# Threshold attention before a squared-ReLU layer: Prelu as the threshold, the exponential behind the turn, and value products with the turned weights as the stationary block

## The chip, the cores and the metric

The kernel runs on one core of one Trainium2 chip. A time is the device time of one execution in microseconds (us), and a kernel's time is the median of its runs. The engines are called PE (TensorE, matrix products; PEld is its loading of stationary blocks), DVE (VectorE), ACT (ScalarE), POOL (GpSimd) and SP (SyncE, which only issues DMAs here). A "fill" below is one LDWEIGHTS, the loading of a stationary block into PE's array; the other operand, which runs through the array, is the streamed one. A "turn" is a transposition done by PE.

## What is computed

```
q, k, v: (8, 8, 576, 64)          # batch, heads, positions, width
scores = q @ k^T / 8
scores = where(scores >= max(scores) - tau, scores, -1e9)       # tau = 0.02
attn   = exp(scores - max(scores));  attn /= (sum(attn) + 1e-9)
x      = (attn @ v), heads side by side: (4608, 512)
h      = max(x @ w_in, 0)                                       # w_in (512, 2048)
out    = (h * h) @ w_out                                        # w_out (2048, 512)
```

The weights w_in and w_out come as 64-bit numbers and are made into 32-bit ones on the chip. Everything else is 32-bit floating point.

## The kernel before

The program has an attention stage and then the two layers, whose products are cut up by a Strassen-like scheme. The change touches the attention stage alone.

Two heads are handled together, one on partitions 0 to 63 and one on 64 to 127 (`j` is the head of the pair). A pair of heads has 576 query rows, which are cut into four blocks of 128 rows and a rest of 64; the rests of two pairs share one block. Each such block is a **unit**, 144 in all, and two units, A and B, make a **period**, 72 in all. The steps of a period are issued in an order written out by hand: `PLAIN` (line 623), `CONVERTING` (line 628) for the periods that also make a block of 32-bit weights (steps c1 to c6), and two lists for the first periods. A dash behind a step's name puts it one period late, so that every engine always has work of several units. Each engine works its instructions off in the order of this list.

For a unit PE multiplies turned q by turned k (`scores`, line 448) into six of the eight PSUM banks, called `sc`: 512 columns and a rest of 64 for each head, cut into blocks of 64 rows and 64 columns of the array, four of which work side by side. DVE copies the negated scores out and takes their minimum on the way (`top`, 475). POOL adds tau (`least`, 483). ACT takes the exponential of the copy (`power`, 486), DVE multiplies it by the threshold's mask and sums it (`mask`, 491), and POOL and DVE make the inverse of the sum (`over`, `inverse`).

The weights of both units must then be turned, since a product sums over partitions. PE turns 18 blocks a period (`fill`, 524) in three parts, V and U into the pool `pt` of two banks and W into banks of `sc`; ACT copies them to the tile `wT` (`filled`, 545). PE also spreads the inverse sums over columns (`spread_sums`, 532). `values` (554) then has a block of V stationary, 64 rows and 64 columns, four side by side, and streams 128 columns of `wT` through it. The product comes out already turned, as the layers want it; ACT and DVE take it out (`values_out`, 701), with the division by the sums there or on POOL (`given_out`, 715).

Turned q and k come from PE as well (`turn`, 414), into banks 1 and 4, with ACT taking them out. q, k and v are asked for by SP some periods ahead. `touch` (378) orders instructions that meet in a PSUM bank.

Of the kernel before, what the change touches and what calls it, by code (L numbers as in the profile page):

```python
# [48 lines left out]
def kernel(  # L49
# [63 lines left out]
    tau_p = const.tile([P, 1], FP32, name="tau_p")  # L113

    def read_tau():
# [4 lines left out]
        nc.vector.tensor_scalar(out=tau_p[:, :], in0=tau_c[:, :], scalar1=0.0, scalar2=None, op0=ALU.max)  # L120
# [250 lines left out]

    touched = deque()
    behind = mybir.DependencyInfo(mybir.DependencyClass.Sync, mybir.DependencyReason.DATA)

    Q_RING, K_RING, W_RING = 3, 4, 2
    MEET = (("scores", "turnedq", (Q_RING,)), ("scores", "turnedk", (K_RING,)), ("last scores", "turnedk", (K_RING,)), ("values", "weights", (W_RING,)), ("last values", "last weights", (W_RING,)), ("x", "weights", (W_RING,)))

    def touch(what, made, at, size, key=0):

        if at is None:  # L380
            return
        on = range(at // BANK, (at + size - 1) // BANK + 1)
        met = {made.ins.engine}
        for kind, other, others, its in reversed(touched):
            e = other.ins.engine
            if e == made.ins.engine:
                continue
            if on[-1] < others[0] or others[-1] < on[0]:
                if any({what, kind} == {x, y} and any((key - its) % n == 0 for n in rings) for x, y, rings in MEET):
# [9 lines left out]
    def half_turn(pt, slot, of, at=None):  # L399

        for r in range(2):
            rows = ds(r * HALF, HALF)
            made = nc.tensor.transpose(pt[:, r, ts(slot, HALF)], of[rows, :], ident[rows, rows])  # L403
            touch("turns", made, at and at + r * BANK, BANK)
# [9 lines left out]
    def turn(i, which, spots, other=None):  # L414
# [5 lines left out]
        for t, x in enumerate(of):  # L420
            for r, (spot, at) in enumerate(spots):
                rows = ds(r * HALF, HALF)
                made = nc.tensor.transpose(spot[:, ts(t, HALF)], x[rows, :], ident[rows, rows])  # L423
                touch("turns", made, at, BANK)
        half, kind = FULL * HALF, "turnedk" if which else "turnedq"

        def scaled(to, spot):
            touch(kind, nc.scalar.activation(out=to, in_=spot[0], func=AF.Identity, scale=qscale[:, :]), spot[1], BANK, i)

        def then():  # L430
            part = lambda r, x, n: (spots[r][0][:, ds(x, n)], spots[r][1])
            if which:
                for r, n in ((0, half), (1, half + REST)):
                    spot = part(r, 0, n)
                    copy_by = other if r and other else nc.scalar.copy
                    touch(kind, copy_by(to[1][:, ds(r * half, n)], spot[0]), spot[1], BANK, i)
                scaled(to[2], part(0, half, REST))
                ask_ahead(i, 1)
            else:
                for r in range(2):  # L440
                    scaled(to[0][:, ds(r * half, half)], part(r, 0, half))
                ask_ahead(i, 0)
# [5 lines left out]
    def scores(n, rest):  # L448
# [3 lines left out]
        for j in range(2):  # L452
            first = n % 2 != j
            to = (3 * j + 1) * BANK + first * (BANK - REST) if rest else (3 * j + 2 * first) * BANK
            for c in range(2):
                rows, at = ds(j * D, D), ds(c * HALF, HALF)
                qT, kT, qR = turned[of[c]]
                lhs = qT[rows, ds((c * FULL + t) * HALF, HALF)] if t < FULL else qR[rows, :]
                made = nc.tensor.matmul(  # L459
                    sc[at, ds(to, count)], lhs, kT[rows, ds(at_k, count)], start=True, stop=True  # L460
                )
                touch("scores" if t < FULL else "last scores", made, to, count, of[c])

    def softmax(n):

        if n // 2 not in smalls:
            smalls[n // 2] = sb.tile([P, 4, 4], FP32, tag="small", bufs=4, name="small")
        small = smalls[n // 2]
        nmx, thr, sm = (small[:, i, ds(n % 2 * 2, 2)] for i in range(3))
        w = sb.tile([P, CH, 2, D], FP32, tag=f"w{n % 4}", name="w")  # L470
        s = sb.tile([P, 2, S], FP32, tag=f"s{n % 2}", name="s")
        weights[n] = w
        of = lambda j: s[:, j, :].rearrange("p (c d) -> p c d", d=D)

        def top(j):
            at = 3 * j * BANK + (n % 2 != j) * (2 * BANK - REST)
            made = nc.vector.tensor_scalar(  # L477
                out=s[:, j, :], in0=sc[:, ds(at, S)], scalar1=1.0, scalar2=None,
                op0=ALU.mult, op1=ALU.min, accum_out=nmx[:, j : j + 1],
            )  # L480
            touch("tops", made, at, S)
# [4 lines left out]
        def power(j):  # L486
            nc.scalar.activation(  # L487
                out=w[:, :, j, :], in_=of(j), func=AF.Exp, bias=nmx[:, j : j + 1], scale=-1.0
            )

        def mask(j):
            nc.vector.scalar_tensor_tensor(  # L492
                out=w[:, :, j, :], in0=of(j), scalar=thr[:, j : j + 1], in1=w[:, :, j, :],
                op0=ALU.is_le, op1=ALU.mult, accum_out=sm[:, j : j + 1],
            )

        def over():
            sm = small[:, 2, :]
            nc.gpsimd.tensor_scalar(out=sm, in0=sm, scalar1=1e-9, scalar2=None, op0=ALU.add)

        def inverse():
            nc.vector.reciprocal(out=small[:, 3, :], in_=small[:, 2, :])

        soft[n] = dict(top=top, least=least, power=power, mask=mask, over=over, inverse=inverse)
# [12 lines left out]
    FIRST = [(u, c) for c in range(CH) for u in range(2)]  # L517
    FILLS = {"V": (0, 8), "W": (8, 2), "U": (10, 8)}
    SCALE_AT = 10

    def weight_at(n):
        return n if n < SCALE_AT else n + 2

    def fill(m, f, pt, at=None):

        first, count = FILLS[f]
        if m not in wT:
            wT[m] = sb.tile([P, (2 * CH + 2) * P], FP32, tag="wT", bufs=W_RING, name="wT")
        for i, (u, c) in enumerate(FIRST[first : first + count]):
            half_turn(pt, i, weights[2 * m + u][:, c, :, :].rearrange("p j d -> p (j d)"), at)  # L530

    def spread_sums(m, pt, at):

        rs, count = smalls.pop(m), FILLS["W"][1]
        for j in range(2):
            for r in range(2):
                rows = ds(r * HALF, HALF)
                for u in range(2):
                    one = rs[rows, 3, 2 * u + j : 2 * u + j + 1]
                    wide = bass.AP(tensor=one.tensor, offset=one.offset, ap=[one.ap[0], [0, D]])  # L540
                    to = pt[ds(u * D, D), r, ts(count + j, HALF)]
                    made = nc.tensor.matmul(to, wide, ident[rows, rows], start=True, stop=True)  # L542
                    touch("turns", made, at + r * BANK, BANK)

    def filled(m, f, pt, at=None, last=False):

        first, count = FILLS[f]
        count += 2 * (f == "W")
        to = wT[m][:, ds(weight_at(first) * P, count * P)]
        copy_by = nc.vector.tensor_copy if last else nc.scalar.copy  # L550
        kind = "last weights" if last else "weights"
        touch(kind, copy_by(joined(to), whole(pt, 0, count)), at, 2 * BANK, m)  # L552

    def values(m):

        for c in range(CH):
            for u in range(2):
                for s, (i, _, count, row) in enumerate(halves(2 * m + u)):
                    for j in range(2):
                        rows = ds(j * D, D)  # L560
                        made = nc.tensor.matmul(  # L561
                            sc[ds(u * D, D), ds(5 * j * BANK + row, count)], loaded_v[i][rows, (c - (u != j)) % CH, :],
                            wT[m][rows, ds(weight_at(2 * c + u) * P + row, count)],
                            start=(c == 0 and s == 0), stop=(c == CH - 1), skip_group_check=True,
                        )
                        part = "first values" if c < FULL else "values" if c == FULL else "last values"
                        touch(part, made, 5 * j * BANK, BANK, m)

    def valued(m):

        for u in range(2):
            n = 2 * m + u
            weights.pop(n)
            if units[n][1] == FULL:
                for i in units[n][0]:
                    loaded_v.pop(i)
                    if i + 3 < len(pairs):
                        load_v(i + 3)
# [839 lines left out]
```

## Time and profile before

| | before |
|---|---|
| median of 3 runs | 1270.58 us (1269.65 to 1272.4) |
| profiled execution, span from first to last instruction | 1273.4 us (its time is not listed apart from the span) |
| PE busy | 1251.7 us, 98% of the span |
| DVE busy | 988.2 us, 78% |
| ACT busy | 844.3 us, 66% |
| POOL busy | 982.5 us, 77% |
| DMA | 196.79 MB, q1's packets 52.8% of 16 engines' span |
| mean granted clock of PE | 0.996 |

The busy shares are means over two unlike stages; a stage is read by itself, from a window of the trace. A row of a line gives the line of the kernel, the engine, the operation, the tiles (written <- read) and the shape: "64*128 64x64" is a stationary block of 64 rows and 128 columns and a streamed operand of 64 partitions and 64 columns. A 32-bit product is recorded as two instructions, a turn as one. Some records of PE can be missing (a few per cent).

### The profile page before, as it was taken

What the parts mean: (1) busy time and instruction counts of PE and PEld (TensorE: products, weight loads), DVE (VectorE), ACT (ScalarE), POOL (GpSimd) and SP (SyncE); (2) the same over time, 40 slices, a digit from 0 to 9 for tenths busy, and PEclk for the clock granted to TensorE, in tenths of its full rate; (3) what the DMA queues carried; (4) which work ended last, traced back from release to release, by engine and by line L of the source; (5) the groups of instructions that cost most, each with busy time, mean ns of one, the idle gap of its engine ahead of it and who ended that gap; (6) DMA issues with size and microseconds to landing.
All of it is one profiled execution on the core that took longest, in us unless ns stands there. A gap on an engine that the chain in (4) does not pass through costs nothing.

```text
span 1273.4 us, 55161 instructions
## 1 busy us (share of the span) xinstructions
PE 1251.7 (98%) x22991; PEld 1093.6 (86%) x22991; DVE 988.2 (78%) x2385; ACT 844.3 (66%) x1536; POOL 982.5 (77%) x1070
## 2 busy tenths in 40 slices
PE   8999999999999999999999999999999999999998
PEld 5777776777777778988888888999999999999998
DVE  6999998999999996886887878867746654665463
ACT  6999998999999994666765856675524432443240
POOL 2999998877776542988898989868787878787776
PEclk8999999999999999999999999999999999999999
DMA  7566677434333323657667657579965336533511
GB/s 186 143 161 154 167 198 188 120 89 107 89 81 89 83 53 97 192 166 237 202 191 231 215 169 249 172 274 369 267 163 152 83 107 163 146 84 107 167 35 35
DMA packets 289912, 196.79 MB, mean 155 GB/s; under 512 B 98560, under 2 KB 250624, under 8 KB 289664
## 3 DMA queue, kind: packets, MB, share of 16 engines
q1 hardware_dynamic: 288352, 192.86, 52.8%
q8 instruction: 181, 2.97, 1.0%
q14 instruction: 67, 0.55, 0.1%
q10 hardware_dynamic: 1312, 0.41, 0.1%
HBM read 120.85 MB, written 72.35 MB: 152 GB/s over the span
## 4 chain that ended last, share of the span: by engine, by line
PE 72%; DMA 3%; ACT 2%; POOL 2%; DVE 1%; issue 1%; DVEq 0%; ACTq 0%; POOLq 0%; SPq 0%
PE po L818 27%; PE ph L997 17%; PE ph L818 10%; PE sc L561 7%; PE sc L459 6%; PE pt L403 4%; PE sc L542 1%; PE sc L423 1%; POOL arena L126 1%; DMA g<-arena 1%; ACT arena L970 1%; DVE arena L126 1%; DMA w<-arena 1%; ACT arena L971 1%; ACT c L857 1%
## 5 line engine op out<-in xcount | busy, mean ns | idle before, releaser
L126 POOL TENSOR_TENSOR arena<-arena 128x512 f32<-128x512 f32 (+1 forms) x314 | 378.7, 1224 | 125.1 <-DVE arena L126 113.5
L818 PE MATMUL po<-wall,arena 128*64 128x128 f32 x7056 | 385.8, 273 | 1.4 <-ACT arena L813 0.8
L818 PEld LDWEIGHTS po<-wall,arena 128*64 128x64 f32 x7056 | 385.1, 137 | 1.9 <-ACT arena L813 1.0
L126 DVE TENSOR_TENSOR arena<-ph,arena 128x512 f32<-128x512 f32 x378 | 254.5, 688 | 77.4 <-PE ph L997 30.9
L123 POOL TENSOR_TENSOR arena<-arena 128x128 f32<-128x128 f32 (+1 forms) x322 | 265.5, 826 | 24.1 <-DMA arena<-w 8.5
L997 PE MATMUL ph<-arena,wall 128*128 128x256 f32 x1176 | 256.7, 380 | 2.3 <-DVE arena L126 2.1
L997 PEld LDWEIGHTS ph<-arena,wall 128*128 128x128 f32 x1176 | 222.4, 190 | 36.3 <-DVE arena L126 6.2
L126 DVE TENSOR_TENSOR arena<-po,arena 128x128 f32<-128x128 f32 x378 | 107.6, 288 | 159.3 <-PE po L818 151.4
L492 DVE SCALAR_TENSOR_TENSOR arena<-arena 128x576 f32<-128x576 f32 x288 | 225.9, 820 | 0.4 <-ACT arena L487 0.3
L487 ACT ACTIVATE arena<-arena 128x576 f32<-128x576 f32 x288 | 214.1, 781 | 13.4 <-DVE arena L477 13.3
L477 DVE TENSOR_SCALAR_CACHE_REDUCE arena<-sc 128x576 f32<-128x576 f32 x288 | 203.4, 752 | 18.5 <-ACT arena L552 5.7
L857 ACT COPY c<-arena 128x512 f32<-128x512 f32 (+1 forms) x295 | 168.9, 578 | 70.1 <-DVE arena L123 36.1
L459 PE MATMUL sc<-arena 64*64 64x512 f32 (+1 forms) x2304 | 179.6, 415 | 5.6 <-ACT arena L552 1.2
L561 PE MATMUL sc<-arena 64*64 64x128 f32 (+1 forms) x5760 | 165.6, 261 | 1.0 <-ACT arena L552 0.5
L123 DVE TENSOR_TENSOR arena<-arena,c 128x512 f32<-128x512 f32 x235 | 154.2, 664 | 12.1 <-ACT c L857 7.1
L561 PEld LDWEIGHTS sc<-arena 64*64 64x64 f32 x5760 | 150.4, 133 | 4.5 <-ACT arena L552 0.7
L552 ACT COPY arena<-pt 128x1024 f32<-128x1024 f32 x143 | 145.0, 1014 | 4.6 <-PE pt L403 3.9
L459 PEld LDWEIGHTS sc<-arena 64*64 64x64 f32 x2304 | 76.8, 134 | 71.4 <-issue 47.2
L813 ACT COPY arena<-po 128x128 f32<-128x128 f32 x63 | 16.6, 264 | 177.6 <-PE po L818 174.8
L818 PE MATMUL ph<-arena,wall 128*64 128x128 f32 x2352 | 129.2, 273 | 0.6 <-DVE arena L710 0.6
L818 PEld LDWEIGHTS ph<-arena,wall 128*64 128x64 f32 x2352 | 128.3, 137 | 1.4 <-issue 1.0
L484 POOL TENSOR_SCALAR arena<-arena,tau_p 128x2 f32<-128x2 f32 x144 | 83.8, 582 | 58.5 <-DVE arena L477 44.7
(55 smaller groups left out, 1142.5 us busy)
## 6 DMA issues: line engine op xcount, KB each, us to landing
gp<-arena SPq DMA_DIRECT2D x96, 256.0 KB, 3.4
arena<-gp SPq DMA_DIRECT2D x96, 256.0 KB, 5.4
w<-arena SPq DMA_DIRECT2D x60, 256.0 KB, 2.7
wall<-w SPq DMA_DIRECT2D x49, 256.0 KB, 5.3
g<-arena SPq DMA_DIRECT2D x48, 256.0 KB, 3.7
arena<-g SPq DMA_DIRECT2D x48, 256.0 KB, 5.0
arena<-w SPq DMA_DIRECT2D x44, 256.0 KB, 3.4
arena<-in_v_dram SPq DMA_DIRECT2D x32, 288.0 KB, 3.8
```

The source lines that it names most:

```text
L123: e.tensor_tensor(out=out, in0=x, in1=y, op=ALU.subtract)
L126: e.tensor_tensor(out=out, in0=x, in1=y, op=ALU.add)
L459: made = nc.tensor.matmul(sc[at, ds(to, count)], lhs, kT[rows, ds(at_k, count)], start=True, stop=True)
L477: made = nc.vector.tensor_scalar(out=s[:, j, :], in0=sc[:, ds(at, S)], scalar1=1.0, scalar2=None, op0=ALU.mult, op1=ALU.min, accum_out=nmx ...
L484: nc.gpsimd.tensor_scalar(out=thr, in0=nmx, scalar1=tau_p[:, :], scalar2=None, op0=ALU.add)
L487: nc.scalar.activation(out=w[:, :, j, :], in_=of(j), func=AF.Exp, bias=nmx[:, j : j + 1], scale=-1.0)
L492: nc.vector.scalar_tensor_tensor(out=w[:, :, j, :], in0=of(j), scalar=thr[:, j : j + 1], in1=w[:, :, j, :], op0=ALU.is_le, op1=ALU.mult, a ...
L552: touch(kind, copy_by(joined(to), whole(pt, 0, count)), at, 2 * BANK, m)
L561: made = nc.tensor.matmul(sc[ds(u * D, D), ds(5 * j * BANK + row, count)], loaded_v[i][rows, (c - (u != j)) % CH, :], wT[m][rows, ds(weigh ...
L818: nc.tensor.matmul(to[cols], lhs[:, cols], rhs, start=start, stop=stop, skip_group_check=True)
L857: nc.scalar.copy(c, y)
L997: nc.tensor.matmul(to[:, 2 * j : 2 * j + 2, :], W_IN[m, k][:, ts(2 * h + j, P)], part_x(steps, k, m), start=(not more and j == 0), stop=Tr ...
```

## The change

- **Threshold.** DVE's `mask` goes. `top` writes the negated scores straight into the weights' tile, and ACT's `keep` puts Prelu in its place: with x = (minimum + tau) - negated score, x stays where it is not negative and is multiplied by 2^80 where it is, which the exponential later makes zero.
- **Exponential.** It is taken when the turned blocks leave PSUM: `filled` is now ACT's Exp with bias -tau instead of a copy. The parts are V (9 - 1 = 8 blocks of unit A), U (8 of unit B) and W (the last block of each, in banks 0 and 5, taken out by two instructions).
- **Value products.** `wT` is now the stationary operand, 64 rows and 128 columns, two blocks side by side, and V with a column of ones is streamed, 65 columns. The result has the query rows on partitions, the sum of the weights in its 65th column, in banks 2 and 3.
- **Division and result.** DVE adds 1e-9 to the sums, takes the inverse and multiplies (`values_out`); the result is turned by PE (`x_turned`, four turns) and taken out by DVE (`x_out`, two copies). `spread_sums`, `over`, `inverse` and POOL's multiplication go.
- **Scores.** The blocks of 64 rows and 64 columns become 64 rows and 128 columns, except in a unit that two pairs share. Units A have banks 1 to 4 and units B banks 0, 1, 4 and 5.
- **Turned q and k** leave PSUM by DVE instead of ACT.
- **V** is loaded with a pitch of 68 numbers, a row of 64 at a time, with ones behind each (set once by POOL for each of three buffers).
- **Order.** New `PLAIN` and `CONVERTING` lists, and a table `NEEDS` that issues a step's forerunners first.

The core of the diff:

```diff
     def load_v(i):
-        va = sb.tile([P, CH, D], FP32, tag="va", bufs=3, name="va")
+        va = sb.tile([P, CH, V_PITCH], FP32, tag="va", bufs=V_RING, name="va")
+        if i < V_RING:
+            nc.gpsimd.memset(va[:, :, D : D + 1], 1.0)
         nc.sync.dma_start(
-            out=va[:, :, :].rearrange("p c d -> p (c d)"),
-            in_=v[b, h : h + 2, :, :].rearrange("j (p c) d -> (j p) (c d)", c=CH),
+            out=va[:, :, 0:D],
+            in_=v[b, h : h + 2, :, :].rearrange("j (p c) d -> (j p) c d", c=CH),
         )
...
-        def scaled(to, spot):
-            touch(kind, nc.scalar.activation(out=to, in_=spot[0], func=AF.Identity, scale=qscale[:, :]), spot[1], BANK, i)
+        def out(to, r, at, count, scale):
+            from_ = spots[:, r, ds(at, count)]
+            if scale:
+                made = nc.vector.tensor_scalar(out=to, in0=from_, scalar1=qscale[:, :], scalar2=None, op0=ALU.mult)
+            else:
+                made = nc.vector.tensor_copy(to, from_)
+            touch(kind, made, banks and banks[r : r + 1], i)
...
+            if t < FULL:
+                qT, kT, _ = turned[of[0]]
+                made = nc.tensor.matmul(
+                    sc[:, ds(to, count)], qT[rows, ts(t, P)], kT[rows, ds(at_k, count)], start=True, stop=True
+                )
+                touch("scores", made, [bank], of[0])
+                continue
...
-        def power(j):
+        def keep(j):
             nc.scalar.activation(
-                out=w[:, :, j, :], in_=of(j), func=AF.Exp, bias=nmx[:, j : j + 1], scale=-1.0
+                out=w[:, :, j, :], in_=w[:, :, j, :], func=AF.Prelu, bias=thr[:, j : j + 1], scale=-1.0, alpha=DROP
             )
-        def mask(j):
-            nc.vector.scalar_tensor_tensor(
-                out=w[:, :, j, :], in0=of(j), scalar=thr[:, j : j + 1], in1=w[:, :, j, :],
-                op0=ALU.is_le, op1=ALU.mult, accum_out=sm[:, j : j + 1],
-            )
...
-        copy_by = nc.vector.tensor_copy if last else nc.scalar.copy
-        touch(kind, copy_by(joined(to), whole(pt, 0, count)), at, 2 * BANK, m)
+        for r in ((slice(0, 2),) if banks is None else (slice(0, 1), slice(1, 2))):
+            made = nc.scalar.activation(
+                out=joined(to)[:, r, :, :], in_=whole(pt, 0, count)[:, r, :, :], func=AF.Exp, bias=below[:, :], scale=1.0
+            )
...
                         made = nc.tensor.matmul(
-                            sc[ds(u * D, D), ds(5 * j * BANK + row, count)], loaded_v[i][rows, (c - (u != j)) % CH, :],
-                            wT[m][rows, ds(weight_at(2 * c + u) * P + row, count)],
-                            start=(c == 0 and s == 0), stop=(c == CH - 1), skip_group_check=True,
+                        sc[ds(row, count), ds((2 + j) * BANK + u * X_PITCH, D + 1)],
+                        wT[m][rows, ds(at + row, count)], loaded_v[i][rows, (c - (u == j)) % CH, 0 : D + 1],
+                        start=(c == 0 and u == 0), stop=(c == CH - 1), skip_group_check=True,
...
+            made = nc.vector.tensor_scalar(
+                out=over(2), in0=both[:, :, :, D], scalar1=1e-9, scalar2=None, op0=ALU.add
+            )
+            nc.vector.reciprocal(out=small[:, 3, :], in_=small[:, 2, :])
+            made = nc.vector.tensor_tensor(
+                out=xn[:, :, :].rearrange("p u (j d) -> p j u d", j=2), in0=both[:, :, :, 0:D], in1=wide, op=ALU.mult
+            )
...
+                for u in range(2):
+                    half_turn(pt["X"], X_SLOT + u, xn[:, u, :], W_BANKS, "x turns", p)
...
+                for r in range(2):
+                    made = nc.vector.tensor_copy(x[:, :, ts(r, HALF)], whole(pt["X"], X_SLOT, 2)[:, r, :, :])
...
     PLAIN = """
-        put give fetch ahead eU-- powA0-- V-- powA1-- eV-- maskA1-- PV-- powB1-- c1- RA- powB0-- T--
-        maskA0-- U- W-- Q-- x-- c4- maskB1-- SA- eT-- RB- maskB0-- topA0- over- topA1- c2 s2 leastA- eW--
-        SB- topB0- s1- c5 c6 topB1- inv- leastB- xm-- c3
+        put give fetch ahead T RA c1 SA zA0- eT tA0 c2 W-- eU-- eW-- tA1 V- c3 SB RB zB1- tB1 c4- lA tB0 lB zB0- eV- c5- P1-- P2--
+        U- out-- c6-- X--- eX--- zA1 s1 s2
     """.split()
     CONVERTING = """
-        put give fetch ahead SB- c1 RA topB0- powA1- c2- topB1- PV- c5- powA0- maskA0- eT- leastB- over- V-
-        x- T powB0- SA RB W- maskA1- c3 c4 inv- Q- c6- topA0 eV- topA1 leastA U xm- maskB0- powB1- eW- eU
-        maskB1- s1 s2
+        put give fetch ahead zA1- c4- zB1- RB eU-- T RA SA W-- eW-- tA0 V- tA1 eT zB0- SB P1-- c1 tB1 lA tB0 eV- zA0 P2-- U- out--
+        lB X--- c3 c6-- c2 eX--- c5- s1 s2
     """.split()
```

In the lists SA, SB, RA and RB are the scores of units A and B, 512 columns and the rest; tA0 and the like the maxima; lA the threshold; zA0 and the like Prelu; V, U and W the turns of the weights and eV, eU, eW their exponentials; P1 and P2 the value products; out the division; X and eX the turned result; T and eT the turns of q or k.

More of the change, by code (lines that the diff above doesn't have):

```diff
@@ L370, in ahead, with touch @@
                 count -= 1
+    Q_RING, K_RING, V_RING, W_RING, X_RING, UNIT_RING = 3, 4, 3, 2, 2, 6
+    V_PITCH = D + 4
+    X_PITCH = D + 2
     touched = deque()
     behind = mybir.DependencyInfo(mybir.DependencyClass.Sync, mybir.DependencyReason.DATA)
[L375 to L380, printed above, removed]
+    MEET = (
+        ("scores", "turnedq", Q_RING), ("scores", "turnedk", K_RING), ("last scores", "turnedk", K_RING),
+        ("values", "weights", W_RING), ("tops", "fills", UNIT_RING), ("sums", "x turns", X_RING),
+    )
+    def touch(what, made, banks, key=0):
+        if banks is None:
             return
-        on = range(at // BANK, (at + size - 1) // BANK + 1)
+        on = frozenset(banks)
         met = {made.ins.engine}
@@ L387, in touch @@
                 continue
-            if on[-1] < others[0] or others[-1] < on[0]:
-                if any({what, kind} == {x, y} and any((key - its) % n == 0 for n in rings) for x, y, rings in MEET):
+            if not on & others:
+                if any({what, kind} == {x, y} and (key - its) % n == 0 for x, y, n in MEET):
                     continue
@@ L412, in joined, with turn @@
         return to.rearrange("p (t r q) -> p r t q", r=2, q=HALF)
-    def turn(i, which, spots, other=None):
+    def turn(i, which, spots, banks=None):
         while any(x[0:2] == (i, which) for x in wanted):
@@ L497, in over @@
[L497 to L504, printed above, removed]
+        soft[n] = dict(top=top, least=least, keep=keep)
     def do(n, what, *args):
@@ L532, in spread_sums @@
[L532 to L549, printed above, removed]
-        copy_by = nc.vector.tensor_copy if last else nc.scalar.copy
[L551 to L561, printed above, removed]
-                            sc[ds(u * D, D), ds(5 * j * BANK + row, count)], loaded_v[i][rows, (c - (u != j)) % CH, :],
-                            wT[m][rows, ds(weight_at(2 * c + u) * P + row, count)],
-                            start=(c == 0 and s == 0), stop=(c == CH - 1), skip_group_check=True,
-                        )
-                        part = "first values" if c < FULL else "values" if c == FULL else "last values"
-                        touch(part, made, 5 * j * BANK, BANK, m)
+    FILLS = {
+        "V": [(0, c) for c in range(FULL + 4)], "U": [(1, c) for c in range(FULL + 4)],
+        "W": [(0, CH - 1), (1, CH - 1)],
+    }
@@ L690, in turn_some @@
         def turn_some():
-            free = None
+            free, banks = spots(), [1, 4]
             if turns and p < 2:
-                pq = pt_pool.tile([P, 2, BANK], FP32, tag="pt", name="pq")
-                free = [(pq[:, r, :], None) for r in range(2)]
-            late["turn"] = [turn(g // 2, g % 2, free or spots()) for g in turns]
-        def PV():
-            if has(2 * m):
-                values(m)
+                free, banks = pt_pool.tile([P, 2, BANK], FP32, tag="pt", name="pq"), None
@@ L767, in step @@
         step(name, p - 1)
+        for other in NEEDS.get(name, "").split():
+            step(other, p)
         made_steps.add((name, p))
```

235 lines of the change are left out of this document (118 added, 117 removed), and 4 rows, old and new, of the table NEEDS.

## The prediction

> **What bounds the kernel now.** I read the page first, then the rows of single lines, then a window of the chain of waits. The page's busy shares, over 40 slices of the span, tell two stages apart.
>
> ```profile
> PE   8999999999999999999999999999999999999998
> DVE  6999998999999996886887878867746654665463
> ACT  6999998999999994666765856675524432443240
> POOL 2999998877776542988898989868787878787776
> PEclk8999999999999999999999999999999999999999
> ```
>
> Up to slice 16 PE, DVE and ACT are all over 90% busy; afterwards only PE is. The rows of a line tell where the first stage begins and ends:
>
> ```profile
> L477 DVE TENSOR_SCALAR_CACHE_REDUCE arena<-sc x288: 720/753/760, 10.1 to 484.3; 128x576 f32<-128x576 f32 x144
> ...
> L561 PEld LDWEIGHTS sc<-arena x5760: 128/133/136, 25.0 to 493.9; 64*64 64x64 f32 x199
> ...
> L818 PEld LDWEIGHTS ph<-arena,wall x2352: 132/137/138, 494.7 to 882.4; 128*64 128x64 f32 x196
> ```
>
> The columns after the count are shortest, median and longest in ns, then first and last start in us. Attention is everything before 494.7 us; the change touches nothing behind it. Four maxima (L477) make a period, 72 periods in all. The last maximum starts about 2.0 us (three times 0.68) after the first of its period, so one period takes (484.3 - 10.1 - 2.0) / 71 = **6.65 us**. Two windows, of the periods without and with weight conversion (columns: length, then busy us of PE, PEld, DVE, ACT, POOL, clock, DMA share), and one period of the chain of waits:
>
> ```profile
> 260.00:450.00 190.00, 189.67 (x5164) 143.04 (x5160) 182.67 (x539) 179.01 (x307) 131.63 (x173) 1.00 0.39 90
> 20.00:250.00 230.00, 222.23 (x5614) 164.36 (x5618) 221.50 (x621) 220.40 (x398) 203.49 (x226) 0.98 0.64 165
> ```
>
> ```profile
> 305.94 2.16 PE sc L561 x67
> 308.11 0.06 PE sc L459
> 308.16 0.07 PE sc L561 x3
> 308.23 0.11 PE sc L459 x6
> 308.34 0.46 PE sc L423 x10
> 308.80 0.50 PE pt L403 x16
> 309.30 0.12 PE sc L403 x4
> 309.42 0.39 PE sc L542 x16
> 309.81 1.85 PE sc L459 x24
> 311.66 0.65 PE pt L403 x16
> 312.31 1.72 PE sc L561 x51
> ```
>
> From value products to value products this period takes 6.37 us (312.31 - 305.94), and the chain is PE's own work without a hole: values 2.2, turned q/k 0.46, turned weights 0.50, 0.12 and 0.65, spread sums 0.39, scores 1.85 and a few short ones. So PE bounds the plain periods, with DVE at 182.67 of 190 us right behind. In the converting stretch all three share the bound at about 0.96 busy. Taking work from DVE or ACT alone can give at most the difference between 6.65 and PE's own 6.4; what the change does to PE decides.
>
> **The change part by part. PE.** The stream rate must be known per shape. In the shape, 64*128 means rows * columns of the stationary block; two blocks of 64*128, or four of 64*64, cover the array.
>
> ```profile
> 301.72 0.58 PEld L403 LDWEIGHTS pt<-ident,arena 64*128 64x128 f32 x16
> ...
> 302.99 0.32 PEld L542 LDWEIGHTS sc<-ident,arena 64*64 64x64 f32 x16
> ...
> 305.87 2.01 PEld L561 LDWEIGHTS sc<-arena 64*64 64x64 f32 x69
> ```
>
> ```profile
> L997 PEld LDWEIGHTS ph<-arena,wall x1176: 186/190/191, 537.7 to 796.1; 128*128 128x128 f32 x196
> L997 PE MATMUL ph<-arena,wall x1176: 378/379/484, 537.7 to 796.3; 128*128 128x256 f32 x196
> ...
> L818 PE MATMUL ph<-arena,wall x2352: 272/273/325, 494.8 to 882.5; 128*64 128x128 f32 x196
> ...
> L403 PEld LDWEIGHTS pt<-ident,arena x2288: 133/139/226, 15.7 to 490.3; 64*128 64x128 f32 x191
> ```
>
> Streaming: 128 more columns cost 379 - 273 = 106 ns, so 128 columns cost 106, 65 cost 54, 512 cost 427. Filling: a matmul's block of 128 columns takes 190 ns, one of 64 columns 137 (133 with 64 rows, so the rows count for nothing): 53 ns per 64 columns, about **107 ns for 128**. The longest matmuls agree, if they are those that had to wait for their own fill: 484 - 379 = 105 with 128 columns, 325 - 273 = 52 with 64.
>
> Value products now: 72 instructions a period (36 products, each recorded twice), four at once, 18 rounds. (2.01 - 0.13) / 17 = 110 ns a round, the streaming of 128 columns; the fill (53) hides behind it. After: again 72, but each fills 64*128 and streams only 65 columns (54 ns), two at once, 36 rounds. If a fill goes on while the previous block streams, a round is the longer of the two, 107 ns, plus what lies between. The turns show that remainder: 16 in 8 pairs, (0.58 - 0.14) / 7 = 63 ns a pair against 53 of streaming, so 8 to 10 ns. I take 115 ns: 36 x 0.115 = 4.14 us against 18 x 0.107 = 1.92, **+2.22 us** a period. No row shows a 64*128 block of a product. From below the price is that of the turns, the same shape in another operation, 63 ns (+0.3 us). From above it is two fills one after the other, 0.214 (+5.8 us), which the turns exclude: 16 fills of 139 ns in 0.58 us overlap. I take the value of the same operation with the same columns (L997), since rows proved indifferent.
>
> The Trainium skill, TensorE: Matmul & The Clock Gate, section LDWEIGHTS (loading the stationary operand), makes a fill proportional to its columns alone, 0.83 ns each, 107 ns for 128 columns. L997 against L818 agrees (53 ns for 64 more), the turns do not (139 ns for 128 columns, as for 64 of a product). By the page the estimate is the forecast; by the turns' row it is the first rival.
>
> The other steps of PE: the score rests (8 instructions a period) become 64*128 as well, 4 rounds of 115 instead of 4 of 63 (spread sums, 16 in fours: (0.32 - 0.13) / 3): +0.21. Scores of 512 columns: 4 rounds of 427 as 16 instructions in fours were, no change (the fill hides behind 427). Spread sums go: -0.39. The turned result X adds 4 turns: +0.13. Entering a group of another shape costs PE time now: the same 16 turns take 0.65 behind 64*64 scores and 0.50 behind turns; likewise 0.46 for 10 turns whose 5 pairs need 0.31, and 2.16 against 1.92 for values. With one shape throughout I count -0.5. Sum: 6.37 + 2.22 + 0.21 + 0.13 - 0.39 - 0.5 = **8.04 us of PE**.
>
> The rows of the other engines that the next steps use:
>
> ```profile
> L487 ACT ACTIVATE arena<-arena 128x576 f32<-128x576 f32 x288 | 214.1, 781 | 13.4 <-DVE arena L477 13.3
> L492 DVE SCALAR_TENSOR_TENSOR arena<-arena 128x576 f32<-128x576 f32 x288 | 225.9, 820 | 0.4 <-ACT arena L487 0.3
> L552 ACT COPY arena<-pt 128x1024 f32<-128x1024 f32 x143 | 145.0, 1014 | 4.6 <-PE pt L403 3.9
> L428 ACT ACTIVATE arena<-sc,qscale 128x256 f32<-128x256 f32 x60 | 25.2, 473 | 0.2 <-DVE arena L477 0.2
> L436 ACT COPY arena<-sc 128x256 f32<-128x256 f32 x31 | 11.5, 370 | 1.3 <-PE sc L423 1.3
> L710 DVE TENSOR_TENSOR arena<-sc,arena 128x128 f32<-128x128 f32 x39 | 10.9, 280 | 2.5 <-PE sc L561 2.5
> L436 DVE COPY arena<-sc 128x320 f32<-128x320 f32 x1 | 0.5, 490 | 2.2 <-PE sc L423 2.2
> L209 ACT ACTIVATE arena<-wall 128x512 f32<-128x512 f32 x32 | 22.4, 701 | 0.0
> L231 DVE TENSOR_SCALAR arena<-arena 128x512 int32<-128x512 int32 x32 | 14.0, 439 | 0.0
> L239 DVE SCALAR_TENSOR_TENSOR wall<-wall,arena 128x512 int32<-128x512 int32 x32 | 21.9, 685 | 0.0
> ```
>
> A new wait comes on top. The fills W stand in banks 0 and 5, which the scores of unit B overwrite; these queue behind ACT's two exponentials on W, with the rests and the value products behind them on PE. From W's end that is about 0.2 to land and two of 0.37 (L428 takes 473 ns for 256 columns, and 128 fewer save 0.84 ns each, by L552 and L436), 0.93 in all; in between PE has the 16 turns of V (0.50, 0.55 with the handover). **+0.38.** So 8.4 with a turn of k, 8.3 over turns of q, k and none. In 16 of 72 periods the unit shared by two pairs halves one unit's blocks to 64*64: 18 of 36 rounds at 115 remain and 18 at 60 come, -1.0. Mean: 8.3 - 0.23 = **8.07 us**.
>
> **DVE and ACT** must stay below that. DVE loses four masks (3.3) and keeps four maxima (2.7). It gains the division (0.15, 0.17, and 256 elements between L710 and L436: 0.42; the small two are guessed), two result copies of 0.28, and the moves of turned q (two of 256, 0.84) or k (256, 320 and 64 elements, 1.1): 5.0 us at most, in converting periods 1.1 more (L231, L239). ACT has four Prelu at the price of the Exp it replaces (781, same shape and operands; no row shows Prelu), two exponentials on 1024 columns (1014 plus the 103 that a scale from memory costs, L428 against L436: 1.12), two on 128 (0.73): 6.1 at most, 6.8 with the conversion's Abs (L209). POOL loses work. All lie beside PE's 8.07. Between the last value product and the next maximum DVE works off the division (0.75), two copies (0.5), the moves (1.0) and two maxima (1.4), 3.7 in all; PE needs some 4.2 from there to its next value products, so this hides with 0.5 to spare and costs the excess if PE gets faster.
>
> **DMA.** V's rows of 2304 bytes become nine of 256: 1024 more packets a load, 32768 in all.
>
> ```profile
> q1 hardware_dynamic: 2619, 1.43, 43.7%
> ```
>
> In the 13 us from 300 on, 2619 packets took 43.7% of 16 engines, 35 ns each, most under 512 B. So 1.15 ms / 16 = 72 us over some 580, a share of 0.12 on top of 0.39 to 0.64: hidden, the loads being asked for two periods ahead. Without that cover, 32 loads would cost a few us each.
>
> **Sum.** 71 x (8.07 - 6.65) = +101. At the end two periods' value products stand behind the last scores, each 2.2 longer: +5. The profile's span of 1273.4 becomes 1379; it lies 2.8 above the median shown, 1270.58, and I add the difference to the median: **1377 us**.
>
> **The rivals.** *Faster:* the fills of 64*128 products cost what those of turns do, 63 ns a round. Then values +0.31, rests nothing, the rest of the sum as above: 6.30, mean 6.2, 71 x (6.2 - 6.65) = -32: **1239**. For it: the identical shape at 139 ns. Against: 190 for 128 columns of a product. The point from which it turns: 0.45 us over some 36 rounds (40 with the rests, less those that shared units save) is 12 ns, so faster below 75 ns a round. *Between:* fills partly hidden, 75 to 95 ns a round: 1271 to 1322. *Far slower:* Prelu and Exp do not share a table, and each change reloads it. In the plain order that is four loads a period.
>
> ```profile
> L1198 ACT ACT_TABLE_LOAD x1 | 1.3, 1283 | 3.3 <-issue 3.3
> ```
>
> 4 x 1.28 + 6.1 = 11.2 us a period on ACT: 71 x 4.55 = +323, **1594**. Against: this one load serves Exp, Copy, Identity, Abs, Relu and Square. The Trainium skill, ScalarE: Activation LUTs, section What ACT_TABLE_LOAD costs, has 2.66 us with the drain; an estimate by that is 16.7 us of ACT a period, while no run here shows a second load.
>
> **How the numbers follow.** Forecast 0.82, faster rival 0.12, between 0.03, table 0.03. Within the forecast the waits decide: PE never waiting (7.7) gives 1350, and with entering still paid and 0.25 more of handovers (8.8) 1428. With fill remainders of 0 to 15 ns the band is **1320 to 1440**; it holds about 0.8 in all. About 0.2% is what a measurement of this kernel can tell from no change. Faster 0.13, same 0.01, slower 0.86.
>
> **What would show it.** Right: LDWEIGHTS of the value products near 190 ns, their group near 4.1 us a period, the chain still PE's, DVE and ACT idle over a fifth of attention, one table load. Wrong: fills of 139 ns, or a group near 2.3 us; then the change is faster. If attention ends near 600 us but the values take 2.3, a wait did it, not the fill.

## The result and the profile after

The changed kernel takes **1392.65 us** (median of 4 runs, 1389.91 to 1393.96), the one before 1271.03 us in the same comparison: a ratio of **1.0945**, 95% interval 1.0918 to 1.0972. It is slower by 122 us. The profiled execution's span is 1390.7 us. The page's busy shares over 40 slices of it:

```profile
PE   8999999999999999999999999999999999999998
PEld 6888888988888888889888888899999999999998
DVE  4766766665555555537868788786774566655663
ACT  4777777766666666636668566586662244322330
POOL 1444444423343322009889898886877788777776
PEclk9999999999999999989999999999999999999999
```

Attention now lasts into the 18th slice instead of the 16th, and in it only PE is full: DVE, ACT and POOL were relieved as intended, and PEld, the fills, went up instead. The rows of single lines of the changed kernel (count, then shortest, median and longest in ns, first and last start in us), the maxima first:

```profile
L495 DVE TENSOR_SCALAR_CACHE_REDUCE arena<-sc x288: 743/752/759, 9.9 to 593.4; 128x576 f32<-128x576 f32 x144
...
L558 PEld LDWEIGHTS sc<-arena x5760: 129/188/335, 25.7 to 611.1; 64*128 64x128 f32 x158, 64*64 64x64 f32 x41
...
L809 PEld LDWEIGHTS ph<-arena,wall x2352: 132/137/232, 613.9 to 1000.0; 128*64 128x64 f32 x196
```

The first layer starts at 613.9 us instead of 494.7: +119.2. From there to the end it is 776.8 us against 778.7, so attention holds the whole difference. The last maximum starts 2.8 us after the first of its period, so a period takes (593.4 - 9.9 - 2.8) / 71 = **8.18 us** instead of 6.65. And the fill of a value product's block (L558) has a median of **188 ns**, where 64*64 blocks had 133. Two stretches of attention and its last 10 us (length, busy us of PE, PEld, DVE, ACT, POOL, clock, DMA share):

```profile
20.00:300.00 280.00, 278.51 (x4908) 245.19 (x4910) 188.47 (x576) 201.28 (x304) 121.27 (x166) 0.99 0.52 138
300.00:590.00 290.00, 289.33 (x5144) 252.59 (x5144) 167.83 (x533) 189.90 (x281) 88.98 (x127) 1.00 0.27 65
...
604.00:614.00 10.00, 7.48 (x122) 6.44 (x124) 2.27 (x10) 1.62 (x3) 0.00 (x0) 0.63 0.07 20
```

DVE is busy 58 to 67% and ACT 65 to 72%. Now the timeline of the fills, in a period with a shared unit and in one without (start, length of the whole group, group):

```profile
355.11 3.60 PEld L558 LDWEIGHTS sc<-arena 64*64 64x64 f32 x108
...
401.76 0.58 PEld L416 LDWEIGHTS pt<-ident,arena 64*128 64x128 f32 x16
402.48 0.72 PEld L470 LDWEIGHTS sc<-arena 64*128 64x128 f32 x5
...
403.78 3.91 PEld L558 LDWEIGHTS sc<-arena 64*128 64x128 f32 x68
```

68 fills in 3.91 us: (3.91 - 0.19) / 33.5 = **0.111 us a pair**, while the same shape as a turn keeps its 63 ns a pair (16 in 0.58). The value products thus take 36 rounds of 0.111 us, 4.0 us, where the period before had 18 rounds of 0.110, 2.0 us. These 2.0 us are more than the period's growth of 1.53; the other steps of PE save the difference. (A group that mixes shapes is named by one of them: the 108 are 72 of 64*64 and 36 of 64*128.)

### The profile page after: what moved, and what is told of

Its sections match the earlier page's. It is cut to its first block, busy times and chain, and to the rows that moved or that the text cites. A ratio compares the mean times of both kernels' runs of the same rounds, so it can differ in the third digit from the quotient of the medians.

```text
span 1390.7 us, 50574 instructions
## 1 busy us (share of the span) xinstructions
PE 1373.6 (99%) x21103; PEld 1263.4 (91%) x21103; DVE 896.8 (64%) x2217; ACT 795.4 (57%) x1345; POOL 834.3 (60%) x929
## 2 busy tenths in 40 slices
DMA packets 322660, 196.50 MB, mean 141 GB/s; under 512 B 135424, under 2 KB 287488, under 8 KB 322432
## 4 chain that ended last, share of the span: by engine, by line
PE 54%; ACT 2%; DVE 0%; DMA 0%; issue 0%; POOL 0%; DVEq 0%; ACTq 0%
PE po L809 28%; PE ph L988 16%; PE ph L809 9%; ACT arena L962 1%; ACT arena L961 1%; PE sc L558 0%; ACT c L848 0%; DVE arena L131 0%; DMA gp<-arena 0%; ACT arena L804 0%; POOL arena L131 0%; DVE arena L705 0%; PE sc L416 0%; DVE arena L685 0%; DVE arena L681 0%
## 5 line engine op out<-in xcount | busy, mean ns | idle before, releaser
L558 PEld LDWEIGHTS sc<-arena 64*128 64x128 f32 (+1 forms) x5760 | 304.0, 179 | 14.9 <-DVE arena L495 8.2
L558 PE MATMUL sc<-arena 64*128 64x65 f32 (+1 forms) x5760 | 308.5, 264 | 0.7 <-ACT arena L542 0.7
L128 POOL TENSOR_TENSOR arena<-arena 128x128 f32<-128x128 f32 (+1 forms) x322 | 265.3, 826 | 20.5 <-DMA arena<-w 4.3
L502 POOL TENSOR_SCALAR arena<-arena,tau_p 128x2 f32<-128x2 f32 x144 | 41.9, 291 | 377.7 <-DVE arena L495 377.7
L542 ACT ACTIVATE arena<-pt,below 128x1024 f32<-128x1024 f32 x144 | 160.2, 1112 | 138.8 <-PE sc L416 74.5
L505 ACT ACTIVATE arena<-arena 128x576 f32<-128x576 f32 x288 | 206.9, 773 | 11.0 <-POOL arena L502 11.0
L470 PE MATMUL sc<-arena 64*128 64x512 f32 (+1 forms) x1024 | 201.3, 454 | 2.0 <-DVE arena L440 1.1
L470 PEld LDWEIGHTS sc<-arena 64*128 64x128 f32 x1024 | 108.9, 189 | 19.7 <-issue 6.8
L681 DVE TENSOR_SCALAR arena<-sc 128x4 f32<-128x4 f32 x72 | 11.7, 162 | 177.5 <-PE sc L558 177.5
```

The costliest lines, as they stand in the source:

```text
L128: e.tensor_tensor(out=out, in0=x, in1=y, op=ALU.subtract)
L470: made = nc.tensor.matmul(sc[:, ds(to, count)], qT[rows, ts(t, P)], kT[rows, ds(at_k, count)], start=True, stop=True)
L502: nc.gpsimd.tensor_scalar(out=thr, in0=nmx, scalar1=tau_p[:, :], scalar2=None, op0=ALU.add)
L505: nc.scalar.activation(out=w[:, :, j, :], in_=w[:, :, j, :], func=AF.Prelu, bias=thr[:, j : j + 1], scale=-1.0, alpha=DROP)
L542: made = nc.scalar.activation(out=joined(to)[:, r, :, :], in_=whole(pt, 0, count)[:, r, :, :], func=AF.Exp, bias=below[:, :], scale=1.0)
L558: made = nc.tensor.matmul(sc[ds(row, count), ds((2 + j) * BANK + u * X_PITCH, D + 1)], wT[m][rows, ds(at + row, count)], loaded_v[i][rows, ...
```

## The experiments

The kernel before the change took 1270.2 to 1271.6 us in the three comparisons. "Pauses" are the times over 0.5 us in which PE ran nothing between 30 us and the last maximum, added up from the trace's records. Every version of the changed kernel has one of 1.42 us among them, a wait for ACT (L505 or L506) between 245 and 305 us. A ratio is to the kernel before.

| run | us | ratio, 95% interval | pauses of PE |
|---|---|---|---|
| before | 1271.03 | | 2, 2.2 us |
| after | 1392.65 | 1.0945 [1.0918, 1.0972] | 1, 1.4 us |
| half blocks in the value products | 1332.6 | 1.0475 [1.046, 1.0491] | 28, 34.9 us |
| V streamed twice | 1408.21 | 1.1073 [1.1057, 1.109] | 1, 1.4 us |
| half blocks, rests too | 1349.99 | 1.0603 [1.0578, 1.0628] | 33, 39.1 us |
| half blocks, all scores too | 1349.62 | 1.0611 [1.0586, 1.0637] | 36, 41.1 us |
| half of the products left out | 1250.97 | 0.9847 [0.982, 0.9873] | 2, 2.0 us |
| before, short streams | 1369.14 | 1.0774 [1.0739, 1.0809] | 53, 59.2 us |
| half rests alone | 1412.15 | 1.1113 [1.1079, 1.1147] | 1, 1.4 us |
| one unit halved | 1369.52 | 1.0785 [1.0753, 1.0816] | 1, 1.4 us |

### Is it the fill?

The theory was that the fill of 128 columns sets the pace of the value products; the rivals were the waits of the new order, the streams, and the plain number of instructions. The first run changes nothing but the width of the stationary blocks:

```diff
-        parts = [halves(2 * m + u) for u in range(2)]
+        parts = [
+            [(i, 0, HALF, row + o) for i, _, count, row in halves(2 * m + u) for o in range(0, count, HALF)]
+            for u in range(2)
+        ]
         of = [(c, u) for c in cs for u in range(2)]
-        if any(len(x) > 1 for x in parts):
-            of.sort(key=lambda x: x[1])
```

> The changed kernel with every 64*128 stationary block of the value products cut into two of 64*64, so 144 instructions a period four at once instead of 72 two at once; the streamed 65 columns, the results and everything else stay. Theory 'fill' (the fill of 128 columns, 0.112 us a round, bounds PE): 36 rounds a period stay, each 0.059 us as in the changed kernel's shared units, so 56 periods x 36 x 0.053 = -107 us, and some +10 for entering another shape: about 1296 us (1285 to 1310). Rival 'waits' (the new order, banks shared by W and X, the exponential on ACT or the longer DVE chain set the period of 8.2 us): no change, 1385 to 1395. Rival 'dispatch' (the count of instructions bounds PE): slower than 1393.

Measured: 1332.6 us, 60 us less than the changed kernel, but 36 more than expected and above the range. The maxima of this run, and its fills in one period:

```profile
L495 DVE TENSOR_SCALAR_CACHE_REDUCE arena<-sc x288: 735/753/759, 9.7 to 538.5; 128x576 f32<-128x576 f32 x144
```

```profile
402.41 2.19 PEld L559 LDWEIGHTS sc<-arena 64*64 64x64 f32 x142
405.86 0.19 PEld L559 LDWEIGHTS sc<-arena 64*64 64x64 f32 x2 [1.26 <-issue]
```

142 fills pass in 2.19 us, 0.059 us for four, as the theory had it: twice the instructions in half the time. "Waits" and "dispatch" as sole causes are out. But then PE stands still for 1.26 us and no semaphore holds it ("issue": it waited for nothing that the profile shows). There are 27 such pauses, 33.5 us together (the 28th of the table is the wait for ACT), nearly the 36 us that are missing. What they are comes below.

The second run doubles the stream and leaves the fill:

```diff
-    X_PITCH = D + 2
+    X_PITCH = 2 * (D + 1)
...
+                    one = loaded_v[i][rows, (c - (u == j)) % CH, 0 : D + 1]
+                    twice = bass.AP(tensor=one.tensor, offset=one.offset, ap=[one.ap[0], [0, 2], [1, D + 1]])
...
-                        sc[ds(row, count), ds((2 + j) * BANK + u * X_PITCH, D + 1)],
-                        wT[m][rows, ds(at + row, count)], loaded_v[i][rows, (c - (u == j)) % CH, 0 : D + 1],
+                        sc[ds(row, count), ds((2 + j) * BANK + u * X_PITCH, X_PITCH)],
+                        wT[m][rows, ds(at + row, count)], twice,
```

> The changed kernel with V streamed twice through each stationary block of the value products (130 columns instead of 65; the second copy goes to PSUM columns that nobody reads). Theory 'fill': a round is the longer of 107 ns of fill and 108 ns of stream, so at most a few ns a round more: 1390 to 1405 us. Rival 'stream' (fill and stream follow each other in a round): +54 ns x 36 rounds x 72 periods = +140, about 1530 us.

Measured: 1408.21 us, some 16 us more than after, just above the theory's range and far from the rival's 1530. The starts of the maxima tell where the 16 us are: an ordinary plain period goes from 8.25 to 8.30 us, one with a shared unit from 7.91 to 8.96. Only there are blocks of 64*64, whose fill is short, and there the longer stream counts. In a 64*128 round a second stream of 54 ns is all but free (0.05 us over 36 rounds, 1 to 2 ns each), so fill and stream do go side by side, and the fill is the longer.

### What would be late without the fill?

This run leaves out half of the products, to see what a period needs when they are short:

```diff
-        of = [(c, u) for c in cs for u in range(2)]
+        whole_ = all(len(x) == 1 for x in parts)
+        of = [(c, u) for c in cs for u in ((0, 1) if c % 2 == 0 else (1, 0))]
...
             for i, _, count, row in parts[u]:
+                row += HALF * ((c + u) % 2) if count > HALF else 0
+                count = HALF
                 for j in range(2):
...
-                        start=(c == 0 and u == 0), stop=(c == CH - 1), skip_group_check=True,
+                        start=(c == 0 and (u == 0 or whole_)), stop=(c == CH - 1), skip_group_check=True,
```

> The changed kernel with only one half (64 columns) of each stationary block of the value products used, in turn the first and the second half, so that half of the products are left out: 72 instructions a period as in the changed kernel, but 64*64 and four at once, 18 rounds of 0.059 us. Theory 'fill' with what is late next: PE falls by 2.9 us a period to about 5.2, below ACT's 6.1 (6.8 in converting periods), so a period of 6.2 to 6.7 and 1265 to 1290 us; no pause of PE for instructions. Rival 'waits' (the new order alone needs 7.3 us, as the run with half blocks seemed to show): about 1330.

Measured: 1250.97 us, 1.5% less than the kernel before and 14 us below the range. Its maxima and two stretches, converting and plain:

```profile
L495 DVE TENSOR_SCALAR_CACHE_REDUCE arena<-sc x288: 740/752/759, 9.3 to 458.7; 128x576 f32<-128x576 f32 x144
```

```profile
20.00:250.00 230.00, 209.59 (x4944) 149.39 (x4940) 221.79 (x575) 201.28 (x303) 131.04 (x164) 0.99 0.64 167
260.00:450.00 190.00, 188.56 (x4788) 150.14 (x4781) 153.53 (x493) 173.30 (x260) 84.77 (x119) 1.00 0.39 93
```

The period is (458.7 - 9.3 - 2.8) / 71 = 6.29 us: 5.70 in most plain periods, by the maxima's starts, where PE is busy for 188.56 of 190 us and ACT for 173.30, and about 6.9 in converting ones, where DVE is the fullest (221.79 of 230). So neither the new order nor ACT's or DVE's work needs 8.2 us; the rival "waits" falls. It also shows that the relief of DVE was real, 154 us busy of 190 against 183 before, and that it is worth nothing while PE's fills are the bound.

### What are the pauses?

Every pause in the run with half blocks but one ends 1.2 to 1.55 us after a packet of the DMA kind "instruction" (16 KB) has landed. If PE runs out of instructions, the old kernel must show it as well when its value products are cut into twice as many, with neither Prelu nor the new order:

```diff
         for c in range(CH):
-            for u in range(2):
-                for s, (i, _, count, row) in enumerate(halves(2 * m + u)):
+            for s in range(2):
+                for u in range(2):
+                    i, count, row = [
+                        (i, HALF, row + o) for i, _, count, row in halves(2 * m + u) for o in range(0, count, HALF)
+                    ][s]
                     for j in range(2):
```

> The kernel before the change with each value product's stream of 128 columns cut in two of 64, so 144 instructions a period instead of 72, four at once, 36 rounds of 0.059 instead of 18 of 0.11 us; nothing else changes, PE's work grows by 0.15 us a period, +10 us. Theory 'instructions' (in the run with half blocks PE paused 35 us in all, each pause ending 1.2 to 1.6 us after an instruction packet had landed, because 288 instructions went by in 2.2 us): such pauses appear here too, some 30 us, so 1300 to 1325. Rival (those pauses belong to the changed kernel's order and waits): 1275 to 1288, no pauses.

Measured: 1369.14 us, +99 us, more than expected. There are 53 pauses, 59.2 us in all (69 with those of 0.1 to 0.5 us, where the kernel before has 8); each ends 1.2 to 1.6 us after an instruction packet. Its fills in one period:

```profile
306.57 2.04 PEld L564 LDWEIGHTS sc<-arena 64*64 64x64 f32 x123
309.56 0.37 PEld L564 LDWEIGHTS sc<-arena 64*64 64x64 f32 x19 [0.95 <-issue]
```

The rounds are 63 ns and not 59, so the products take 2.3 us without a pause against 2.0: 0.3 us x 72, some 22 us, where 10 were expected. With 61 us more of pauses that makes 83 of the 99 us; the other 16 stay open. The pauses thus do not belong to the changed kernel. No row names what PE waits for, but the records do tell. Queue q8 brings packets of 16384 bytes, 217 in this run for 55720 records of PE (the sequencer's included), 202 for 51890 in the run with half blocks and 181 for 46504 in the kernel before: one for 257 records each time. Counted through those records, all 53 pauses of this run, the 27 of the run with half blocks and both of the kernel before stand at the same place of a block of 256, behind the 193rd record. The wait for ACT stands elsewhere. So PE waits for its next block of instructions. The Trainium skill, Runtime: NRT & Kernel Launch, section Instruction fetch mechanics, says that each engine's instruction memory is refilled in blocks of 16 KiB, 256 instructions, by a queue of its own, and that the cost of a block is mostly hidden. The size and the count agree; hidden it is, but for 2.2 us, at 144 instructions (72 fills and 72 matmuls) in 2 us, as in the kernel before, and no longer at 284 to 288 in 2.0 to 2.3 us, where about one pause of 1.1 to 1.25 us comes every 1.4 periods (this run) to 2.6 (half blocks in the changed kernel).

> The changed kernel with the value products of unit A alone in 64*64 halves, unit B in 64*128 blocks: 108 instructions a period. Theory 'fill': 18 rounds at 0.112 and 18 at 0.059, -0.95 us x 56 = -53, with an entry of 0.1 to 0.15 about 1345 to 1350. Theory 'instructions': the burst of 144 instructions in 1.1 us stays below a packet of 256, so pauses of PE near none. Rival 'waits': the next limit is met, 1393 less than half of 53 saved.

```diff
         parts = [halves(2 * m + u) for u in range(2)]
+        if all(len(x) == 1 for x in parts):
+            ((i, _, _, _),) = parts[0]
+            parts[0] = [(i, 0, HALF, 0), (i, 0, HALF, HALF)]
```

Measured: 1369.52 us, 23 less than after where 43 to 48 were expected, and no pauses but the wait for ACT, at 285 us. Less than half of 53 is saved, as the rival "waits" had it; the row of the fills says otherwise. One period's:

```profile
406.83 3.60 PEld L561 LDWEIGHTS sc<-arena 64*64 64x64 f32 x108
```

3.60 us, to the digit what shared units take in the changed kernel. The two shapes should need 18 x 0.111 + 18 x 0.059 = 3.06; both shapes lie in each of the two parts P1 and P2, so PE passes from one to the other four times a period, and the 0.54 us are put down to that, 0.135 each; the next run prices such an entry by itself. A plain period fell from 8.25 to 7.90 us, by nearly what the group fell, from 4.0 to 3.60, so no other limit was met.

### What does another shape cost?

```diff
-            if t < FULL:
+            if t < FULL and not rest:
                 qT, kT, _ = turned[of[0]]
...
-                    sc[ds(c * HALF, HALF), ds(to, count)], qR[rows, :], kT[rows, ds(at_k, count)],
+                    sc[ds(c * HALF, HALF), ds(to, count)], lhs, kT[rows, ds(at_k, count)],
```

> The changed kernel with the score rests (64 streamed columns) in 64*64 blocks, everything else as changed. By the fill alone 4 rounds from 0.112 to 0.06: -0.2 us x 64 = -13, 1380. If entering a group of another shape costs PE 0.15 us, as the sum of the prediction had it, two groups of rests a period cost four entries, +0.6 - 0.2 = +0.4 x 64 = +26: about 1418. No change (1390 to 1396) would mean that an entry costs about 0.05.

Measured: 1412.15 us. The maxima:

```profile
L496 DVE TENSOR_SCALAR_CACHE_REDUCE arena<-sc x288: 745/753/759, 9.7 to 615.0; 128x576 f32<-128x576 f32 x144
```

A period is 8.49 us, +0.31; with the 0.2 that the rests save, four entries cost 0.5, **0.13 us each**. The 0.2 is worked out from the prices of the rounds, not measured. The price in the prediction's sum was about 0.15.

The same edit on top of the half blocks, and then all scores in halves (`if t < FULL and False`):

> As the run with half blocks in the value products, and the score rests (64 streamed columns) in 64*64 blocks as before the change too. Theory 'fill': 4 rounds a period from 0.112 to 0.06, -0.2 us x 64 = -13 against the run with half value blocks, less where PE must enter another shape once more: 1275 to 1300 us. Rival: the rests lie beside something else, no change against that run.

> As the run before, with the 512-column scores in 64*64 blocks four at once too. Streaming is the same in both shapes and the fill hides behind 427 ns, so theory 'fill' expects no change by itself; with one entry into another shape less or more a period (0.15 us), within 11 us of the run with half rests. Whether it lies below 1271, the kernel before the change, decides what the rest of the change is worth.

Measured: 1349.99 and 1349.62 us, 17 us slower than with half value blocks alone. The first expectation missed: it had seen only the fill, and the added entries (and 4 us more of pauses) outweigh it. The second held, no difference between the two. No version of the changed kernel that computes all its products came below the one before: half value blocks without their pauses for instructions would stand at 1332.6 - 33.5, about 1299, an estimate.

## Why the prediction was right

1377 us were forecast, within 1320 to 1440, and 1392.65 measured, by the mechanism that was named. Several smaller terms were off, and in part they cancel. Step by step:

- **Fill of 128 columns, 107 ns and 8 between, 115 a round: right.** 111 measured, fills of 188 ns, 4.0 us a period against 4.14. That a turn of the same shape needs about half the time a round, and that rows do not count, was read rightly from L997, L818 and L403. The Trainium skill, TensorE: Matmul & The Clock Gate, section LDWEIGHTS (loading the stationary operand), has a fill go by columns alone. The products agree (188 ns recorded for 128 columns, 133 for 64), the turns do not, as before: 63 ns a pair next to 111.
- **First rival (fills as cheap as turns), 1239:** out, by the row of L558. (By its own prices its values add 0.35, 36 x 0.063 - 1.92, and not 0.31: 1242.) **Third (tables reloaded):** out; one load of the table, and Prelu takes what Exp took. The rows of the changed kernel:

```profile
L542 ACT ACTIVATE arena<-pt,below 128x1024 f32<-128x1024 f32 x144 | 160.2, 1112 | 138.8 <-PE sc L416 74.5
...
L505 ACT ACTIVATE arena<-arena 128x576 f32<-128x576 f32 x288 | 206.9, 773 | 11.0 <-POOL arena L502 11.0
...
L1189 ACT ACT_TABLE_LOAD x1 | 1.3, 1283 | 3.3 <-issue 3.3
```

- **Entering another shape, -0.5 a period:** supported, 0.13 an entry by the run with half rests; that run adds entries, and no run takes out exactly those that the change does.
- **New wait behind W's exponentials, +0.38: between 0.14 and 0.40.** W's exponentials are two instructions, one for each bank. Unit B's scores in bank 0 (L470 at 402.48) wait for the first alone and start 0.14 us after the last turn of V would have let the next group start (401.76 + 0.58); those in bank 5 wait for the second, as the sum had it for both, and start at 402.74, 0.40 after. The two halves of PE's array then run apart, and start level only at a unit A's scores (400.73 and 400.74). No run tells how much of the lag the period pays.
- **Scores of 512 columns, "no change": too small.** The first of a unit's two rounds takes 0.49 to 0.53 us in the changed kernel (400.73 to 401.27, 402.48 to 403.02), and 0.43 to 0.48 before, where 0.427 was reckoned for every round. These are 0.427 and a fill of 128 columns (0.107) or of 64 (0.053): the fill is not wholly hidden there. That is 0.1 to 0.2 us a period.
- **Shared units, -1.0 in 16 periods: too large, the mis-sized term.** 3.60 us for the products instead of the 3.15 it implied, since the entries between the shapes inside the group had been left out. Worth +0.5 x 16, 8 us. By the maxima's starts a plain period with a shared unit took 7.91 us, 0.6 above the 7.3 of the sum, and the others 8.24 to 8.39, at the 8.3 of the sum. There the cheaper values (-0.14) and the dearer scores cancel in part, which is luck. The mean came out at 8.18 against 8.07, +8 us over 71 periods.
- **End of attention, +5: too small.** The last maximum starts at 593.4 and the layer at 613.9, 20.5 us, against 10.4 before (484.3 to 494.7): +10. With no scores left to fill the gaps PE waits between products, and in the last 10 us its granted clock is 0.63, which the prediction had not seen; what each of the two costs is not separated.
- **DVE and ACT beside PE: right** (58 to 72% busy). DVE's terms add up to 5.1 and not 5.0, and both prices were a little high: its 188.47 us of 280, mostly converting, are 5.5 us a period where 6.1 were reckoned, its 167.83 of 290 are 4.7. In the run with half of the products DVE takes 0.96 of 6.9, 6.7 us, because the conversion's two instructions take longer there (L244 1432 ns instead of 681, L236 880 instead of 418, means from 30 to 230 us); no run shows why.
- **DMA: right.** 322660 packets instead of 289912, 32748 more where 32768 were counted, V's loads land in 4.2 us (median) instead of 3.8, and no wait on them stands out.

The remaining 2 to 3 us are bookkeeping: the profiled span lay 2.8 us above the median before and lies 1.95 below it after, and the layers took 1.9 us less.

## What to carry to other kernels

When a product's operands are swapped, count the columns that must be filled, those that are streamed, and how many blocks work side by side. Before, a round of four blocks took 0.110 us for 128 streamed columns; after, a round of two took 0.111 for 128 filled ones, with 65 or 130 streamed alike. So the roles cost a factor of two although the arithmetic stayed the same. Price a fill from a row of the same operation, not of the same shape, since turns and products differ. And relief of an engine that is nearly as full as the bound (DVE, 183 to 154 us of 190 in the run with half of the products) pays only if the change leaves the bound itself alone.

## What the runs showed of the hardware

PE can run out of instructions. With 72 matmuls and 72 fills of value products a period (144 instructions in 2 us) it paused 2.2 us from 30 us on to the last maximum; with 288 instructions in 2.1 to 2.3 us it paused 33.5 to 59 us, every pause at the same place of a block of 256 instructions and ending 1.2 to 1.6 us after a 16 KB packet of instructions landed. Cutting products smaller to fill the array better was therefore worth 60 us instead of some 94.

Four 64*64 blocks side by side take 59 ns a round, fill and 65 streamed columns included, so 15 ns a matmul; two of 64*128 take 111. And a group of another shape costs 0.13 us to enter (0.5 us for four entries with the rests in halves, 0.54 with one unit halved).
